# Attention and feed-forward on one core: the general path, which is passed over, takes its scores in three matmuls of 256 keys in place of two of 384

## The chip, the cores and the metric

The kernel runs on one core of a Trainium2 chip. A core has five engines that work beside each other, each with its own stream of instructions: TensorE (PE, matmuls and, as PEld, their weight loads), VectorE (DVE), ScalarE (ACT), GpSimd (POOL) and SyncE (SP, which issues transfers). They wait for each other through semaphores. The metric is the device time of one execution in microseconds (us), lower is better.

## The reference, cut to what matters

Four batches, eight heads, 768 positions, 64 numbers per head. Three of the eight heads see every earlier key; the other five see only the first four keys and a window of the last 64. The attention's output is joined over the heads to rows of 512 and goes through a feed-forward part that takes the maximum of two products.

```python
scores = scale * np.matmul(q, k.transpose(0, 1, 3, 2))
mask = np.where(retr, full_mask, stream_mask)          # per head
scores = np.where(mask, scores, -1000000000.0)
a = np.exp(scores - np.max(scores, axis=-1, keepdims=True))
a = a / (np.sum(a, axis=-1, keepdims=True) + 1e-09)
x = np.matmul(a, v)                                    # joined over heads: 3072 x 512
out = np.maximum(x @ w1, x @ w2) @ w_out
```

## The kernel before, in words

The kernel holds two programs for the same result.

The **fast path** (`tile_three_full_heads`) is written for three full heads and five windowed ones. It reads from `is_retrieval` which heads these are, sorts them, and addresses them through registers. Each batch is worked in two halves of 384 queries. For a half the queries and keys are cast and turned (L712), scores are made in blocks of 128 keys by 128 queries (L893), ScalarE takes the exponential (L912), VectorE masks it (L931), and TensorE multiplies with the values (L956). VectorE divides by the sums (L973, L983). The feed-forward part follows: w1 - w2 is formed once (L1122), its product with x is taken (L1177) and clipped at zero (L1201), and an output product adds this times w_out to x times a product of w2 and w_out (L1227). ScalarE or VectorE copies a tile of results (L480, L482), and a transfer stores it (L1246). The order of all this is not that of the text: a planner (`Order.run`) simulates the engines with given costs and emits the instructions in the order that it finds.

The fast path does not subtract the row's maximum before the exponential. So it ends with a judgement: VectorE checks that all reciprocal sums lie between 1e-12 and 1e12, TensorE adds up the checks (L1296), and VectorE (L1300 to L1307) writes one number, `verdict`, which is 1 if all are good and three heads are full.

The **general path** (`tile_any_heads`, from L1318 on) computes everything anew for any heads and any sums. For each batch, head and block of 128 queries it makes the scores of all 768 keys: matmuls into a tile of sums (L1407), each followed by a multiplication by scale and mask on VectorE (L1411). Then come the maximum, the exponential, the product with the values, and the feed-forward part.

What joins the two stands at the end of the program. Each engine loads the verdict into a register (L1581), and compares it (L1584):

```python
        right = nc.values_load(
            verdict, min_val=0, max_val=1, skip_runtime_bounds_check_because="a product of two flags"
        )
    with tc.If(right < 1):
        tile_any_heads(tc, *anyhow)
```

With verdict 1, as for the inputs used here, each engine jumps over the instructions of the general path. In its place stands a short block, also under L1584: it adds to the semaphores of the engines what the passed-over instructions would have added. Then comes the closing barrier (L1621, the line that opens the whole program): SP waits for all transfers and engines, each engine drains, GpSimd collects them and releases them, clears the semaphores, and once more collects and releases.

In each engine's stream the instructions stand in this order: fast path, general path, the short block, the closing barrier. TensorE passes over 9,803 instructions, VectorE over 3,165, GpSimd over 256, ScalarE over 136, and SP over one.

Of the kernel before, what the change touches and what calls it, by code (L numbers as in the profile page):

```python
# [11 lines left out]
F32 = mybir.dt.float32  # L12
# [1307 lines left out]
def tile_any_heads(tc, q, k, v, is_retrieval, w1, w2, wo, out, n_sink, window):  # L1320

    nc = tc.nc
    B, H, S, D = q.shape
# [3 lines left out]
    scale = 1.0 / float(D) ** 0.5  # L1327
# [8 lines left out]
        name="any_mask_table",  # L1336
# [5 lines left out]
    ps_s = pool("any_ps_s", 1, space=PSUM)  # L1342
# [9 lines left out]
        out=raw,  # L1352
# [9 lines left out]
    for name, src in (("any_w1", w1), ("any_w2", w2), ("any_wo", wo)):  # L1362
        n, cols = src.shape[0] // 128, src.shape[1]
# [9 lines left out]
    for b in range(B):  # L1373
        x = work.tile([128, NB, d_model], BF16, tag="x", name="any_x")
        for h in range(H):
            turned = []
            for name, src in (("any_q", q), ("any_k", k)):
                f = work.tile([128, NB, D], F32, tag="f", name="any_f")
                nc.gpsimd.dma_start(out=f, in_=src[b, h].rearrange("(n p) d -> p n d", p=128))
                fb = work.tile([128, NB, D], BF16, tag="fb", name="any_fb")  # L1380
                nc.vector.tensor_copy(out=fb, in_=f)
                pt = ps_t.tile([128, 1024], BF16, tag="t", name="any_pt")
                for i in range(NB):
                    nc.tensor.transpose(pt[0:D, i * 128:(i + 1) * 128], fb[:, i], ident)
                ft = work.tile([D, S], BF16, tag=name, name=name)
                nc.vector.tensor_copy(out=ft, in_=pt[0:D, 0:S])
                turned.append(ft)
            qt, kt = turned
            f = work.tile([128, NB, D], F32, tag="f", name="any_f")
            nc.gpsimd.dma_start(out=f, in_=v[b, h].rearrange("(n p) d -> p n d", p=128))  # L1390
            vb = work.tile([128, NB, D + 1], BF16, tag="vb", name="any_vb")
            nc.vector.memset(vb[:, :, D:D + 1], 1.0)
            nc.vector.tensor_copy(out=vb[:, :, 0:D], in_=f)
            for i in range(NB):
                if i % 3 == 0:
                    s3 = work.tile([128, 3, S], F32, tag="s", name="any_s")
                    a3 = work.tile([128, 3, S], BF16, tag="a", name="any_a")
                s = s3[:, i % 3]
                ps = ps_s.tile([128, 2, 512], F32, tag="s", name="any_ps")
                m = work.tile([128, S], F32, tag="m", name="any_m")  # L1400
                nc.vector.scalar_tensor_tensor(
                    out=m, in0=masks[:, 1, i], scalar=r[:, h:h + 1], in1=masks[:, 0, i],
                    op0=ALU.mult, op1=ALU.add,
                )
                for e in range(2):
                    cols = slice(e * S // 2, (e + 1) * S // 2)
                    nc.tensor.matmul(  # L1407
                        ps[:, e, 0:S // 2], lhsT=qt[:, i * 128:(i + 1) * 128], rhs=kt[:, cols],
                        start=True, stop=True,
                    )  # L1410
                    nc.vector.scalar_tensor_tensor(  # L1411
                        out=s[:, cols], in0=ps[:, e, 0:S // 2], scalar=scale, in1=m[:, cols],
                        op0=ALU.mult, op1=ALU.mult,
                    )
                nc.vector.tensor_scalar(
                    out=m, in0=m, scalar1=1e9, scalar2=-1e9, op0=ALU.mult, op1=ALU.add
                )
                nc.vector.tensor_tensor(out=s, in0=s, in1=m, op=ALU.add)
                top = work.tile([128, 1], F32, tag="top", name="any_top")
                nc.vector.tensor_reduce(out=top, in_=s, op=ALU.max, axis=AX.X)  # L1420
                nc.vector.tensor_scalar(
                    out=s, in0=s, scalar1=top, scalar2=None, op0=ALU.subtract
                )
                if i % 3 < 2:
                    continue
                nc.scalar.activation(out=a3, in_=s3, func=ACT.Exp)
                for n in range(3):
                    pt = ps_t.tile([128, 1024], BF16, tag="t", name="any_pt")
                    for j in range(NB):
                        nc.tensor.transpose(  # L1430
                            pt[:, j * 128:(j + 1) * 128], a3[:, n, j * 128:(j + 1) * 128], ident
                        )
                    at = work.tile([128, S], BF16, tag="at", name="any_at")
                    nc.vector.tensor_copy(out=at, in_=pt[:, 0:S])
                    po = ps_o.tile([128, 512], F32, tag="o", name="any_po")
                    for j in range(NB):
                        nc.tensor.matmul(
                            po[:, 0:D + 1], lhsT=at[:, j * 128:(j + 1) * 128], rhs=vb[:, j],
                            start=(j == 0), stop=(j == NB - 1),
                        )  # L1440
                    z = work.tile([128, 1], F32, tag="z", name="any_z")
                    nc.vector.tensor_scalar(
                        out=z, in0=po[:, D:D + 1], scalar1=1e-9, scalar2=None, op0=ALU.add
                    )
                    nc.vector.reciprocal(out=z, in_=z)
                    nc.vector.tensor_scalar(
                        out=x[:, i - 2 + n, h * D:(h + 1) * D], in0=po[:, 0:D], scalar1=z, scalar2=None,
                        op0=ALU.mult,
                    )
        for i in range(NB):  # L1450
            pt = ps_t.tile([128, 1024], BF16, tag="t", name="any_pt")
            for kc in range(KC):
                cols = slice(kc * 128, kc * 128 + 128)
                nc.tensor.transpose(pt[:, cols], x[:, i, cols], ident)
            xt = work.tile([128, KC, 128], BF16, tag="xt", name="any_xt")
            nc.vector.tensor_copy(out=xt, in_=pt[:, 0:d_model].rearrange("p (c t) -> p c t", c=KC))
            g = work.tile([128, FC, 128], BF16, tag="g", name="any_g")
            for fc in range(FC):
                both_ = []
                for wb in (w1b, w2b):  # L1460
                    ph = ps_o.tile([128, 512], F32, tag="o", name="any_ph")
                    for kc in range(KC):
                        nc.tensor.matmul(
                            ph[:, 0:128], lhsT=wb[:, kc, fc * 128:(fc + 1) * 128], rhs=xt[:, kc],
                            start=(kc == 0), stop=(kc == KC - 1),
                        )
                    both_.append(ph)
                h1 = work.tile([128, 128], F32, tag="h1", name="any_h1")
                nc.vector.tensor_copy(out=h1, in_=both_[0][:, 0:128])
                nc.vector.tensor_tensor(out=g[:, fc], in0=both_[1][:, 0:128], in1=h1, op=ALU.max)  # L1470
            pout = ps_o.tile([128, 512], F32, tag="o", name="any_pout")
            for fc in range(FC):
                nc.tensor.matmul(
                    pout, lhsT=g[:, fc], rhs=wob[:, fc], start=(fc == 0), stop=(fc == FC - 1)
                )
            ot = work.tile([128, d_model], F32, tag="ot", name="any_ot")
            nc.vector.tensor_copy(out=ot, in_=pout)
            r0 = b * S + i * 128
            nc.gpsimd.dma_start(out=out[r0:r0 + 128, :], in_=ot)
# [39 lines left out]
def kernel(  # L1519
# [19 lines left out]
    if not (1 <= window <= 64 and 0 <= n_sink <= 64):  # L1539
        tile_any_heads(tc, *anyhow)  # L1540
        return
# [42 lines left out]
    with tc.If(right < 1):  # L1584
        tile_any_heads(tc, *anyhow)
# [40 lines left out]
```

## Time and profile before

| what | value |
|---|---|
| median of three runs | 184.38 us |
| the three runs | 184.38, 184.33, 184.59 us |
| the profiled execution's own time | 183.78 us |
| its span, from the first to the last instruction | 180.9 us |
| mean granted clock of TensorE | 0.999 |
| verdict written (L1307) | 153.7 us after the span's start |
| last copy of results begins (L480) | 177.44 us |

The profile is of one execution. Its span is a little shorter than its time, since the time also takes in what lies around the first and last instruction. An engine is counted as busy while it computes; jumps, waits and the issuing of transfers are not counted as busy, but the view of a source line shows them with an engine's name and a q (PEldq, DVEq and so on), their durations, and when the first and the last of them began. The chain of waits is followed back from the last instruction that counts as work.

### The profile page before, as it was taken

What the parts mean: (1) busy time and instruction counts of PE and PEld (TensorE: products, weight loads), DVE (VectorE), ACT (ScalarE), POOL (GpSimd) and SP (SyncE); (2) the same over time, 40 slices, a digit from 0 to 9 for tenths busy, and PEclk for the clock granted to TensorE, in tenths of its full rate; (3) what the DMA queues carried; (4) which work ended last, traced back from release to release, by engine and by line L of the source; (5) the groups of instructions that cost most, each with busy time, mean ns of one, the idle gap of its engine ahead of it and who ended that gap; (6) DMA issues with size and microseconds to landing.
All of it is one profiled execution on the core that took longest, in us unless ns stands there. A gap on an engine that the chain in (4) does not pass through costs nothing.

```text
span 180.9 us, 4911 instructions
## 1 busy us (share of the span) xinstructions
PE 171.1 (95%) x1816; PEld 106.2 (59%) x1836; DVE 96.7 (53%) x283; ACT 131.7 (73%) x287; POOL 42.8 (24%) x77
## 2 busy tenths in 40 slices
PE   7899599989999999999999999999999999999992
PEld 7767486466747656565545565565466645545561
DVE  3456796599788985576247476656448500000000
ACT  3399695597999999999996984677798524525421
POOL 0000710100609488799671000000000000000000
PEclk9999999999999999999999999999999999999999
DMA  5999999999999999999999999160151052012013
GB/s 139 323 253 336 343 224 242 344 298 278 254 297 273 323 293 284 150 250 217 147 102 136 236 173 200 66 145 0 62 145 62 0 145 116 11 58 116 0 60 125
DMA packets 74929, 32.67 MB, mean 181 GB/s; under 512 B 54162, under 2 KB 71826, under 8 KB 74898
## 3 DMA queue, kind: packets, MB, share of 16 engines
q1 hardware_dynamic: 54704, 28.71, 64.9%
q0 software_dynamic: 19904, 3.41, 26.4%
q8 instruction: 16, 0.26, 0.6%
q10 hardware_dynamic: 290, 0.16, 0.3%
q14 instruction: 15, 0.12, 0.2%
HBM read 25.46 MB, written 6.29 MB: 176 GB/s over the span
## 4 chain that ended last, share of the span: by engine, by line
PE 73%; SPq 11%; DMA 6%; ACT 3%; DVE 3%; issue 2%; DVEq 0%; ACTq 0%
PE ps L1227 32%; PE ps L1177 24%; PE ps L893 7%; PE ps L956 7%; DMA ld<-in_v_dram 6%; SPq L523 5%; SPq L608 4%; PE ps L712 3%; ACT at L912 2%; SPq L513 2%; DVE w L1122 1%; SPq L595 1%; ACT qk L480 1%; DVE vx L482 1%; DVE vb L482 0%
## 5 line engine op out<-in xcount | busy, mean ns | idle before, releaser
L912 ACT ACTIVATE at<-ps 128x512 bf16<-128x512 f32 (+2 forms) x134 | 64.9, 595 | 3.5 <-PE ps L893 1.9
L1177 PE MATMUL ps<-xt,w 128*128 128x384 bf16 x256 | 46.0, 326 | 0.9 <-DVE w L1122 0.6
L1227 PE MATMUL ps<-wob,g 128*128 128x512 bf16 (+1 forms) x192 | 45.3, 370 | 0.4
L1177 PEld LDWEIGHTS <-w 128*128 128x128 bf16 x256 | 23.5, 98 | 15.9 <-issue 0.9
L1201 ACT ACTIVATE g<-ps 128x384 bf16<-128x384 f32 x56 | 27.5, 503 | 7.0 <-PE ps L1177 6.5
L931 DVE TENSOR_TENSOR at<-at,tab 128x1024 bf16<-128x1024 bf16 (+5 forms) x49 | 25.5, 537 | 12.7 <-ACT at L912 12.4
L1227 PEld LDWEIGHTS <-g 128*128 128x128 bf16 x200 | 18.1, 98 | 17.6 <-issue 0.2
L480 ACT COPY ot<-ps 128x512 f32<-128x512 f32 (+1 forms) x20 | 11.4, 572 | 22.8 <-PE ps L1227 22.7
L1227 PE MATMUL ps<-w2o,xt 128*128 128x512 bf16 (+1 forms) x91 | 24.2, 370 | 0.6
L956 PEld LDWEIGHTS <-at 128*128 128x128 bf16 x477 | 19.8, 97 | 7.3 <-issue 0.2
L983 DVE TENSOR_TENSOR x<-ps,rez 128x192 f32 x64 | 22.8, 356 | 1.8 <-DVE x L983 0.2
L956 PE MATMUL ps<-vb,at 128*128 128x65 bf16 x387 | 21.6, 193 | 0.0
L893 PE MATMUL ps<-qk 64*128 64x128 bf16 (+1 forms) x322 | 20.1, 230 | 0.3
L482 POOL CAST qb<-ld 128x384 bf16 x23 | 11.9, 551 | 35.5 <-DMA ld<-in_k_dram 35.5
L893 PEld LDWEIGHTS <-qk 64*128 64x128 bf16 x322 | 11.9, 94 | 11.2 <-issue 8.2
L1227 PEld LDWEIGHTS <-xt 128*128 128x128 bf16 x100 | 9.2, 98 | 8.8 <-issue 0.2
L480 ACT COPY qk<-ps 128x768 bf16<-128x768 bf16 x17 | 12.9, 817 | 0.6 <-PE ps L712 0.6
L471 PE MATMUL ps<-warmer 128*128 128x128 bf16 x147 | 12.1, 250 | 1.1 <-POOL warmer L1564 1.1
L712 PE MATMUL ps<-tab,qb 128*128 128x128 bf16 x144 | 10.4, 219 | 2.9 <-POOL qb L482 2.1
L480 ACT CAST qb<-ld 128x384 bf16 (+1 forms) x23 | 8.8, 452 | 5.1 <-DMA ld<-in_k_dram 3.1
L471 PEld LDWEIGHTS <-warmer 128*128 128x128 bf16 x147 | 10.9, 115 | 1.4 <-POOL warmer L1564 1.1
L712 PEld LDWEIGHTS <-qb 128*128 128x128 bf16 x144 | 8.4, 98 | 4.0 <-POOL qb L482 2.7
(62 smaller groups left out, 146.1 us busy)
## 6 DMA issues: line engine op xcount, KB each, us to landing
out_dram<-ot SPq DMA_DIRECT2D x23, 256.0 KB, 2.3
ld<-in_q_dram SPq DMA_DIRECT2D x6, 768.0 KB, 6.8
ld<-in_k_dram SPq DMA_DIRECT2D x6, 768.0 KB, 7.7
ld<-in_v_dram SPq DMA_DIRECT2D x18, 256.0 KB, 6.7
ld<-in_moe_w_dram SPq DMA_DIRECT2D x8, 512.0 KB, 8.2
wob<-in_moe_w_out_dram POOLq DMA_DIRECT2D x4, 256.0 KB, 8.5
ld<-in_q_dram POOLq DMA_DIRECT2D x8, 96.0 KB, 7.0
ld<-in_k_dram POOLq DMA_DIRECT2D x8, 96.0 KB, 7.2
```

The lines of the kernel that those rows point to most:

```text
L471: nc.tensor.matmul(banks[e][:, 0:128], lhsT=warm, rhs=warm, start=True, stop=True)
L480: nc.scalar.copy(out=out, in_=in_)
L482: eng[e].tensor_copy(out=out, in_=in_)
L712: nc.tensor.transpose(to[:, i], qbs[:, T["qb", n, hf] % NQB, t, i].rearrange("p h d -> p (h d)"), ident)
L893: nc.tensor.matmul(to.rearrange("p (i c) -> p i c", c=128), lhsT=lhsT, rhs=q_of(n, i, m)[rows], start=bk not in under, stop=True, skip_gro ...
L912: nc.scalar.activation(out=at[:, bk, 0:w], in_=bank(("ps", b, hf, t), part=bk)[:, 0:w], func=ACT.Exp, scale=scale,)
L931: eng[e].tensor_tensor(out=at, in0=at, in1=tbl, op=ALU.mult)
L956: nc.tensor.matmul(po[:, hh, i - NT * hf, :], lhsT=ats[:, T["at", b, hf, t] % NAT, bk, e * 128:(e + 1) * 128], rhs=rhs, start=first, stop= ...
L983: nc.vector.tensor_tensor(out=xs[:, (2 * b + hf) % NX, :, bass.ds(heads[2 * p + hh], 1), :], in0=po[:, hh, :, 0:D].unsqueeze(2), in1=z[:, ...
L1177: nc.tensor.matmul(bank(key)[:, 0:HALF], lhsT=w[:, kc, fc * 128:(fc + 1) * 128], rhs=xts[:, (2 * b + hf) % NXT, :, kc, :], start=(kc == 0) ...
L1201: nc.scalar.activation(out=g, in_=ph, func=ACT.Relu)
L1227: nc.tensor.matmul(bank(key)[:, cols], lhsT=lhsT, rhs=(w2o if kind == "x" else wob)[:, c, cols], start=(e == 0), stop=(e == len(steps) - 1),)
```

## The change

In the general path, the scores of a block of 128 queries are made in three pieces of 256 keys in place of two of 384. The tile of sums has the same size as before, 1024 numbers in each of 128 partitions; before, each half of 384 began at a multiple of 512, now the three pieces of 256 stand side by side in the first 768.

```diff
-                ps = ps_s.tile([128, 2, 512], F32, tag="s", name="any_ps")
+                ps = ps_s.tile([128, 1024], F32, tag="s", name="any_ps")
...
-                for e in range(2):
-                    cols = slice(e * S // 2, (e + 1) * S // 2)
+                for e in range(3):
+                    cols = slice(e * S // 3, (e + 1) * S // 3)
                     nc.tensor.matmul(
-                        ps[:, e, 0:S // 2], lhsT=qt[:, i * 128:(i + 1) * 128], rhs=kt[:, cols],
+                        ps[:, cols], lhsT=qt[:, i * 128:(i + 1) * 128], rhs=kt[:, cols],
                         start=True, stop=True,
                     )
                     nc.vector.scalar_tensor_tensor(
-                        out=s[:, cols], in0=ps[:, e, 0:S // 2], scalar=scale, in1=m[:, cols],
+                        out=s[:, cols], in0=ps[:, cols], scalar=scale, in1=m[:, cols],
                         op0=ALU.mult, op1=ALU.mult,
                     )
```

The general path is emitted 4 x 8 x 6 = 192 times for a block of queries, so the program holds 192 more matmuls, 192 more weight loads and 192 more multiplications on VectorE, all behind the comparison of L1584.

## The prediction

> **What bounds the kernel now.** I read the page's header and its chain first, then asked for the lines that the diff touches, then followed the last microseconds through the end of the timeline and the views of the source lines that close the program. The page:
>
> ```profile
> span 180.9 us, 4911 instructions
> PE 171.1 (95%) x1816; PEld 106.2 (59%) x1836; DVE 96.7 (53%) x283; ACT 131.7 (73%) x287; POOL 42.8 (24%) x77
> ...
> PE 73%; SPq 11%; DMA 6%; ACT 3%; DVE 3%; issue 2%; DVEq 0%; ACTq 0%
> PE ps L1227 32%; PE ps L1177 24%; PE ps L893 7%; PE ps L956 7%; DMA ld<-in_v_dram 6%; SPq L523 5%; SPq L608 4%; PE ps L712 3%; ACT at L912 2%; SPq L513 2%; DVE w L1122 1%; SPq L595 1%; ACT qk L480 1%; DVE vx L482 1%; DVE vb L482 0%
> ```
>
> TensorE is busy for 95% of the span and carries 73% of the chain, through the two output products (L1227, L1177). Before them stands a piece that waits for loads (DMA and SPq, 17%). Every line named lies in the fast path. The view of the source line of the changed matmul says:
>
> ```profile
> nothing on L1407; most used: ['L956', 'L893', 'L1227', 'L1177', 'L712', 'L471', 'L482', 'L912', 'L480', 'L983', 'L569', 'L1138', 'L1156', 'L1201', 'L931', 'L1246', 'L1086', 'L973', 'L1621', 'L523', 'L867', 'L1607', 'L513', 'L583', 'L1584']
> ```
>
> So the changed matmul isn't executed, and no line between L1318 and L1466 is among the most used. The end of the timeline, and from the view of the transfers the issue of the last store:
>
> ```profile
> 177.44 0.37 ACT L480 COPY ot<-ps 128x256 f32<-128x256 f32 x1 [0.89 <-PE ps L1227]
> 177.85 0.35 ACTq L1246 DMA_DIRECT2D out_dram<-ot  x1
> ```
> ```profile
> out_dram<-ot ACTq DMA_DIRECT2D x1, 128.0 KB, 1.8
> ```
>
> The last copy is followed by the last store, issued at 177.85 and landed 1.8 us on, at about 179.65. Beside that runs a second thing, the passing over itself. This is the view of L1584, the condition (start times in the fourth column):
>
> ```profile
> L1584 POOLq EVENT_SEMAPHORE  x4: 17/43/43, 157.0 to 157.3; - x4
> L1584 POOLq COMPARE_BRANCH  x1: 45/45/45, 154.2 to 154.2; - x1
> L1584 DVEq COMPARE_BRANCH  x1: 72/72/72, 154.3 to 154.3; - x1
> L1584 POOLq INC_SWDGE_SEM  x1: 422/422/422, 157.3 to 157.3; - x1
> L1584 DVEq EVENT_SEMAPHORE  x1: 21/21/21, 157.3 to 157.3; - x1
> L1584 PEldq COMPARE_BRANCH  x1: 3660/3660/3660, 175.9 to 175.9; - x1
> L1584 SPq COMPARE_BRANCH  x1: 53/53/53, 177.6 to 177.6; - x1
> L1584 ACTq COMPARE_BRANCH  x1: 54/54/54, 178.6 to 178.6; - x1
> L1584 ACTq EVENT_SEMAPHORE  x1: 17/17/17, 179.3 to 179.3; - x1
> L1584 PEldq EVENT_SEMAPHORE  x1: 51/51/51, 179.6 to 179.6; - x1
> ```
>
> Every engine evaluates the condition and jumps over the general path. SP, which has next to nothing to jump over, needs 53 ns. GpSimd stands from 154.2 to 157.0 and VectorE from 154.3 to 157.3; TensorE, which has by far the most to jump over, needs 3660 ns, from 175.9 to 179.6. Whether that matters is read from the closing barrier (L1621):
>
> ```profile
> L1621 SPq EVENT_SEMAPHORE  x14: 17/28/28, 177.8 to 180.8; - x14
> ...
> L1621 SPq DRAIN  x3: 7/7/13, 180.0 to 180.3; - x3
> L1621 DVEq DRAIN  x2: 10/14/17, 157.5 to 180.3; - x2
> L1621 ACTq DRAIN  x2: 8/8/8, 179.4 to 180.3; - x2
> L1621 PEldq DRAIN  x2: 8/8/8, 179.8 to 180.3; - x2
> ```
> ```profile
> SPq L1621 <- DMA out_dram<-ot: 1.5, 2, 1.2
> ```
>
> VectorE comes to the barrier at 157.5, ScalarE at 179.4, TensorE at 179.8, and SP, which first waits for the last store, at 180.0. So the store ends the program, and TensorE's jump is hidden behind it with only about 0.2 us to spare (two times rounded to 0.1, so 0.1 to 0.3). VectorE has 22.5 us to spare.
>
> **The change part by part.** In the program as built, the instructions ahead of the jump stand in the same order on all five engines, ScalarE, GpSimd and SP have the same number everywhere, and only the numbering of temporary registers differs. Behind the jump TensorE has 384 instructions more in the block that is passed over (192 matmuls and 192 weight loads: 4 batches x 8 heads x 6 blocks of queries, one more piece each) and VectorE 192 more. The terms:
>
> 1. Work executed: none added, none removed, 0 us. No queue, buffer, transfer or wait ahead of L1584 moves.
>
> 2. Constants that count the work passed over: in the branch not taken, TensorE and VectorE each add to a semaphore what the passed-over block would have added (4896 becomes 5088, 2754 becomes 2946), and two of SP's closing waits ask for values larger by 192. These four instructions are executed in both kernels, with another constant each: the 51 ns and 21 ns of L1584 and two of the 17 to 28 ns waits of L1621. Same number, same kind: 0 us.
>
> 3. The jump: TensorE's reaches 384 instructions further, VectorE's 192. What a longer jump costs, no row shows, so I bound it. From below: TensorE's could become as cheap as SP's (53 ns in place of 3660), and TensorE would stand at the barrier 3.6 us earlier; the store still lands when it does, so the span gains 0. From above: the price grows with the distance. Between SP's 53 ns over almost nothing and TensorE's 3660 ns over some 9,800 instructions, that is 0.37 ns each, or 0.14 us for 384 more, which is within the 0.2 us of cover. I take 0, because GpSimd passes over 256 instructions and takes 2.8 us (154.2 to 157.0) while VectorE passes over 3,165 and takes 3.0 us: past the first few hundred instructions the distance hardly counts. VectorE's own term is 0 at either end, with 22.5 us of cover. If TensorE's cover were gone, each further microsecond of its jump would be a microsecond of the program.
>
> 4. Placement: the code gets larger, and other data may come to lie elsewhere. No row shows an address. Its nearest measure is the spread of the three runs, 184.33 to 184.59: I allow 0.13 us to either side and take 0.
>
> Sum: 0 + 0 + 0 + 0 against the profiled execution's own 183.78 us, of which the span is 180.9 and 2.9 lie around it. The median of the runs shown, 184.38, is 0.60 above that execution; moved by the same sum it is **184.38 us**.
>
> The instruction queues on the page and, second, in the window from 177 to 181 us (packets, MB, share of the 16 transfer engines):
>
> ```profile
> q8 instruction: 16, 0.26, 0.6%
> ```
> ```profile
> q8 instruction: 2, 0.03, 3.4%
> q14 instruction: 2, 0.02, 1.3%
> ```
>
> Queue q8 brings code in pieces of 0.26 MB / 16 = 16 KB, and one takes 0.6% x 16 engines x 180.9 us / 16 = 1.09 us. Two of them fall in the last 4 us, so TensorE's long jump is a fetch of the code behind it, and another piece follows. [...]
>
> **The rivals.**
>
> *A border between two pieces of code falls just behind the landing (slower).* TensorE executes six instructions from its landing to the end: the semaphore of L1584, a jump, and two drains with two waits of L1621. If a border between pieces falls among them, TensorE must wait for one more piece before or inside the barrier, and everything waits for TensorE. Its price lies between one piece, 1.09 us, and a whole jump, 3.66 us, each less the 0.2 us of cover: 0.9 to 3.4 us. The nearest row is the whole jump, since VectorE's 3.0 us also show that most of a fetch is not the transfer: 184.38 + 3.4 = 187.8 us (185.3 at the low end). It decides from the point where TensorE's first drain comes after 180.0. For it: 384 more instructions move the landing, and the cover is thin. Against it: the landing can hit few places out of many; of the three long landings in this trace (TensorE, VectorE, GpSimd) none shows a second gap of that kind. 6 in 100.
>
> *Code behind the landing now arrives sooner (faster).* The last q8 piece could be one for which TensorE waits after the span, in the 2.9 us that lie around it. If that wait went, up to one piece would be saved: 184.38 - 1.1 = 183.3 us. For it: two q8 pieces lie in the last 4 us. Against it: inside the span it can gain nothing, as the store is later than TensorE; what lies around the span, no row shows. 6 in 100.
>
> *The change does reach executed work.* Were the general path run, its lines would stand in the profile. These rows price it, from the groups and from the groups of the last 6 us:
>
> ```profile
> L1177 PE MATMUL ps<-xt,w 128*128 128x384 bf16 x256 | 46.0, 326 | 0.9 <-DVE w L1122 0.6
> ```
> ```profile
> L1227 PE MATMUL ps<-wob,g 128*128 128x256 bf16 x16 | 2.1, 273 | 0.0
> ```
>
> Three matmuls of 256 columns take 3 x 273 = 819 ns, two of 384 take 2 x 326 = 652 ns: 192 x 167 ns = 32 us more on TensorE, 216 us were it all exposed. Nothing on L1407 speaks for it. 1 in 100.
>
> *Placement beyond the spread*, in either direction: 1 in 100, slower at 184.9.
>
> **How the numbers follow.** No measurable change 0.86 (within 0.2% of 184.38, 0.37 us, about what a measurement of this kernel can tell from no change); border behind the landing 0.06; general path reached 0.01; placement 0.01; code sooner 0.06. So faster 0.06, same 0.86, slower 0.08. The likeliest time is 184.38. The range from 184.0 to 184.8 holds the first case, with the 0.14 us of a jump that grows with its distance and the 0.13 us of placement; the 14 in 100 outside it may be left out.
>
> **What would show it.** If each step is right, the profile after has the same count of instructions on each engine, nothing on the lines of the general path, TensorE's jump near 3660 ns, its first drain before SP's, and the chain on the same lines with the same shares. The first rival would show as a TensorE drain or semaphore of L1621 or L1584 later than SP's with a further q8 piece before it. The second would show as an unchanged span with less around it. A jump that grows with the distance would show as about 3.8 us. I am wrong if the median leaves 184.0 to 184.8.

## The result, and the profile after

The changed kernel takes 183.31 us (median of 14 runs, 182.82 to 183.95) against 184.41 us before (median of 14, 183.59 to 185.78). The ratio is 0.9934, 95% interval 0.9914 to 0.9954: 0.66% faster, where no change was forecast. A second set of 10 runs gave 0.9937, 0.9907 to 0.9966. Two executions further on, of 187.79 us (VectorE +192) and 186.22 us (no general path), lie over 1.5% above the fastest of their kernel and are left out of its medians and ratio.

Of the profile after, the header and the engines' row:

```profile
span 181.5 us, 4931 instructions
PE 171.9 (95%) x1836; PEld 105.8 (58%) x1836; DVE 96.4 (53%) x283; ACT 131.8 (73%) x287; POOL 43.1 (24%) x77
```

The busy times are those of before to within 0.7%; the 20 additional TensorE rows are records that the trace before lacks. The span is *longer* than before, 181.5 against 180.9 us, and yet the profiled execution's own time is shorter, 183.38 against 183.78 us. So the gain isn't in the span at all. What lies around the span, time less span, went from 183.78 - 180.9 = 2.9 us to 183.38 - 181.5 = 1.9 us. It stands at 1.8 to 2.0 us in each of the 14 runs after. Below, "around the span" always means this difference.

The line of the condition (L1584) and the closing barrier (L1621), after:

```profile
L1584 DVEq COMPARE_BRANCH  x1: 72/72/72, 154.6 to 154.6; - x1
L1584 DVEq EVENT_SEMAPHORE  x1: 21/21/21, 157.5 to 157.5; - x1
...
L1584 PEldq COMPARE_BRANCH  x1: 3957/3957/3957, 176.3 to 176.3; - x1
L1584 SPq COMPARE_BRANCH  x1: 53/53/53, 177.9 to 177.9; - x1
...
L1584 PEldq EVENT_SEMAPHORE  x1: 51/51/51, 180.3 to 180.3; - x1
```
```profile
L1621 SPq DRAIN  x3: 7/7/13, 180.6 to 180.9; - x3
...
L1621 PEldq DRAIN  x2: 8/8/8, 180.4 to 181.0; - x2
...
L1621 PEldq EVENT_SEMAPHORE  x2: 51/51/51, 180.8 to 181.4; - x2
```

TensorE's jump is not shorter (3957 ns against 3660), and TensorE still comes to the barrier 0.2 us ahead of SP. Inside the span nothing was won.

### The profile page after: what moved, and what is told of

Its sections match the earlier page's. It is cut to its first block, busy times and chain, and to the rows that moved or that the text cites. A ratio compares the mean times of both kernels' runs of the same rounds, so it can differ in the third digit from the quotient of the medians.

```text
span 181.5 us, 4931 instructions
## 1 busy us (share of the span) xinstructions
PE 171.9 (95%) x1836; PEld 105.8 (58%) x1836; DVE 96.4 (53%) x283; ACT 131.8 (73%) x287; POOL 43.1 (24%) x77
## 4 chain that ended last, share of the span: by engine, by line
PE 60%; SPq 15%; DMA 14%; DVE 6%; ACT 2%; issue 1%; POOL 1%; POOLq 0%; DVEq 0%
PE ps L1227 29%; PE ps L1177 18%; DMA ld<-in_v_dram 7%; SPq L523 6%; PE ps L956 6%; PE ps L893 6%; DMA ld<-in_k_dram 4%; SPq L608 3%; SPq L513 3%; DMA ld<-in_q_dram 3%; DVE w L1122 3%; PE ps L712 1%; DVE vx L482 1%; SPq L595 1%; ACT at L912 1%
## 5 line engine op out<-in xcount | busy, mean ns | idle before, releaser
L1227 PE MATMUL ps<-wob,g 128*128 128x512 bf16 (+1 forms) x200 | 46.8, 371 | 0.0
L1227 PE MATMUL ps<-w2o,xt 128*128 128x512 bf16 (+1 forms) x100 | 24.8, 370 | 0.1
```

Of the source, the lines that this page charges most:

```text
L1227: nc.tensor.matmul(bank(key)[:, cols], lhsT=lhsT, rhs=(w2o if kind == "x" else wob)[:, c, cols], start=(e == 0), stop=(e == len(steps) - 1),)
```

## The experiments

The span of single executions wanders (for the kernel before from 180.8 to 182.4 us over 26 runs). What lies around it wanders too, from 2.6 to 3.3 us in the same runs, but stays well clear of the 1.8 to 2.0 us after the change. So each kernel is judged by that as well as by its time. Theory A: it matters where TensorE lands within the pieces in which its code arrives (on queue q8 before, 16 of 16 KB); before the change a border between pieces stands just behind the kernel's last instructions, and TensorE waits there, after the span. Rival B: the same on VectorE. Rival C: a larger program lies elsewhere in memory.

In all but the kernel without the general path and the two with a late store, only the passed-over part of the kernel before was altered; its result, had it been run, would have been the same. TensorE's part is made longer by repeating a matmul in N of the 192 blocks of queries, which adds 2N instructions (a weight load and a matmul each) to TensorE and none to the others:

```diff
                         start=True, stop=True,        # the matmul of L1407, in the kernel before
                     )
+                    if e and (b * H + h) * NB + i < N:
+                        nc.tensor.matmul(
+                            ps[:, e, 0:S // 2], lhsT=qt[:, i * 128:(i + 1) * 128], rhs=kt[:, cols],
+                            start=True, stop=True,
+                        )
                     nc.vector.scalar_tensor_tensor(
```

### Which engine's passed-over part, and has the step a period?

Four kernels on one chip: TensorE alone as in the change (N = 192, 384 instructions), VectorE alone as in the change, TensorE by 256 (N = 128), and no general path. The edits of the second and the fourth (`spare` is a single number, set up beside the verdict):

```diff
                 nc.vector.tensor_tensor(out=s, in0=s, in1=m, op=ALU.add)
+                nc.vector.tensor_copy(out=m, in_=s)
```
```diff
     with tc.If(right < 1):
-        tile_any_heads(tc, *anyhow)
+        nc.vector.memset(spare, 0.0)
```

> Only TensorE's passed-over part grows, by 384 instructions as in the change; VectorE's stays at 3,165. Theory A (the place where TensorE lands within its pieces of code sets what lies behind the span): as after, 183.3 us, with 1.9 us around the span. Rival B (VectorE's landing does it): as before, 184.4 us, 2.9 us around the span. Rival C (a larger program lies elsewhere in memory): something between or beyond, with no fixed 1.0 us.

> Only VectorE's passed-over part grows, by 192 instructions as in the change; TensorE's stays at 9,803. Theory A: as before, 184.4 us, 2.9 us around the span. Rival B: as after, 183.3 us, 1.9 us. Rival C: no fixed step.

> TensorE's passed-over part grows by 256 instructions, one whole piece of 16 KB if an instruction takes 64 bytes. Theory A: the landing keeps its place within the piece, so the time is as before, 184.4 us with 2.9 us around the span, although the program is larger. If only a longer jump or a larger program counts (rival C): nearer to after, 183.3 to 183.7 us.

> The general path is left out: what stands under the condition is one clearing of a number, so only the fast path's result is computed. Theory A: every engine's jump becomes short (TensorE's 3660 ns to about 50 to 100 ns), the last store still ends the span, near 181 us; around the span 1.9 us if no border follows the new landing, so 182.5 to 183.3 us. Rival C: the same span, but no telling what lies around it. If TensorE's jump were hidden for good, the span would not shorten by more than 0.3 us.

| kernel | runs | time, us | ratio to before, 95% | median span | around the span |
|---|---|---|---|---|---|
| before, same chip | 26 | 184.23 | | 181.25 | 2.9 |
| TensorE +384 | 6 | 182.89 | 0.9920 (0.9879 to 0.9962) | 181.2 | 1.7 |
| VectorE +192 | 9 | 184.40 | 1.0013 (0.9984 to 1.0041) | 181.3 | 3.1 |
| TensorE +256 | 10 | 184.10 | 0.9998 (0.9971 to 1.0025) | 181.15 | 2.9 |
| no general path | 8 | 182.98 | 0.9929 (0.9905 to 0.9953) | 181.3 | 1.7 |

TensorE's part alone makes the gain, VectorE's alone doesn't: rival B falls. Making the program larger by 256 instructions changes nothing: rival C falls too, and the step has a period that divides 256. The median spans differ by at most 0.15 us, so the spans carry none of the 1.2 us.

Without the general path, these are the condition (L1585 there) and the barrier (L1622):

```profile
L1585 PEldq COMPARE_BRANCH  x1: 223/223/223, 176.8 to 176.8; - x1
```
```profile
L1622 SPq DRAIN  x3: 7/7/13, 180.8 to 181.1; - x3
...
L1622 PEldq DRAIN  x2: 13/645/1277, 177.1 to 181.2; - x2
```

TensorE's jump falls from 3660 to 223 ns (50 to 100 had been expected) and it stands at the barrier 3.7 us ahead of SP, with a median span of 181.3 against 181.25 us: inside the span the jump was indeed hidden behind the last store.

### Where is the border?

Eight more values of N: the kernel with 128 more ran four times, the other seven once each.

> TensorE passes over 128 instructions more than before, so it lands at the same place within a piece of 256 as with 384 more, in a smaller program. Theory A: as after, 1.6 to 2.0 us around the span, about 183.1 us. Rival C: like the kernel with 256 more, 2.9 us, 184.1 us.

> 32 instructions more. Theory A says that the code that TensorE executes behind its landing reaches over a border; with 32 more the landing is either still ahead of that border (2.9 us around the span) or already behind it (1.7 us). Only if the border stands within the first six instructions behind the landing would the span itself grow, by 0.9 to 3.4 us.

> 64 instructions more: ahead of the border 2.9 us around the span, behind it 1.7 us; together with the kernel of 32 more it places the border to within 32 instructions.

> 192 instructions more, which is 64 short of a whole piece. Theory A: 2.9 us around the span if TensorE executes more than the distance from here to the next border (up to 64 more instructions than before are needed to stay ahead of it), 1.7 us if fewer. It bounds how much TensorE executes behind the landing.

> 8 instructions more than before. The border that 32 more pass lies less than 32 instructions behind the landing's place with 0 more. If it is still ahead: 2.9 us around the span. If it is passed: 1.7 us. If it stands within TensorE's six instructions between landing and end: the span itself grows, TensorE's drain comes after SP's wait for the store, and 185 to 188 us result.

> 16 instructions more: as for 8 more, one of three: 2.9 us around the span (border ahead), 1.7 us (border passed), or a span longer by 0.9 to 3.4 us (border within the six instructions).

> 24 instructions more: one of the same three. With 8 and 16 more, the border is placed to within eight instructions.

> 240 instructions more, 16 short of a whole piece: the landing lies 16 instructions further ahead of the border than before. 192 more, 64 further ahead, gave 1.7 us around the span, 256 more gave 2.9. If what TensorE executes reaches the border early enough to wait for it: 2.5 to 2.9 us; if it comes to it so late that the next piece is there: 1.7 us; between the two if the wait shrinks with the distance.

| TensorE's part longer by | time, us | span | around the span |
|---|---|---|---|
| 0 (before, profiled) | 183.78 | 180.9 | 2.9 |
| 8 | 184.18 | 182.4 | 1.8 |
| 16 | 183.30 | 181.6 | 1.7 |
| 24 | 182.94 | 181.2 | 1.7 |
| 32 | 182.86 | 181.2 | 1.7 |
| 64 | 182.84 | 181.2 | 1.6 |
| 128 (4 runs) | 182.69 | 181.0 | 1.7 |
| 192 | 185.16 | 183.5 | 1.7 |
| 240 | 183.07 | 181.4 | 1.7 |
| 256 (10 runs) | 184.10 | 181.15 | 2.9 |

With 128 more the ratio is 0.9912 (0.9886 to 0.9938). The wait exists only in a narrow stretch: at 0 and at 256, and no longer at 240 or at 8. A single execution can tell this, since around the span there were never under 2.5 us in the runs with 0 or 256 more, and never over 2.0 us in those of the other kernels of this table or after the change. The kernels with 8, 16, 24 and 240 more ran on another chip, where the kernel before, run once, took 183.73 us with 2.9 us around the span. The two times over 184 us with 1.7 to 1.8 us around the span are single executions in which TensorE came to its jump 1.0 and 2.6 us later than in the profile before; one execution can't tell more of these.

### Is it a wait in time, and can it be brought into the span?

Two kernels hold back the last store by six copies on ScalarE, one with TensorE's program untouched and one with 128 more. A third adds 4 instructions (N = 2). The fourth is the changed kernel once more, beside these on one chip.

```diff
+    late = keep.tile([128, d_model], F32, name="late")
...
                 def store(_, number=number, i=i, cols=cols, ends=ends):
                     r0 = b * S + i * 128
+                    for _ in range(6 if ends else 0):
+                        nc.scalar.copy(out=late, in_=ots[:, number % NOUT])
```

> The kernel before with six more copies on ScalarE ahead of the last store, which come to 3.4 us; TensorE's program is untouched and lands when it did, so the next piece of code, which starts some 0.7 us behind the landing and takes 1.1 us, is there before the barrier opens. Theory A as a wait in time: the span grows by about 3.4 us and 1.7 us stand around it, so 186.3 us. If the place has a fixed price: 2.9 us around the span, 187.5 us.

> The same late store with TensorE's passed-over part 128 instructions longer: by either reading 1.7 us around a span of about 184.6 us, 186.3 us. It is the scale for the kernel with the late store alone: equal to it if the border is a wait in time, 1.2 us less if it is a fixed price.

> 4 instructions more than before. 0 more waits behind the span, 8 more does not wait. If the border stands just behind TensorE's six last instructions, 4 more bring it in among them: TensorE would wait inside the barrier, the span would grow by 1 to 3 us (182.5 to 184.5 us) and 1.7 us stand around it. If the border is further on, 2.9 us around an unchanged span.

> The changed kernel beside the others on one chip. If VectorE's 192 more count for something: 1.9 us around the span, against 1.7 us in the kernels in which TensorE's part alone grew. If that was a difference between chips: 1.7 us.

| kernel | runs | time, us | ratio to before, 95% | median span | around the span |
|---|---|---|---|---|---|
| before, same chip | 21 | 184.37 | | 181.4 | 3.0 |
| late store | 6 | 186.12 | 1.0094 (1.0064 to 1.0123) | 184.45 | 1.7 |
| late store, TensorE +128 | 2 | 186.81 | 1.0115 (1.0053 to 1.0178) | 185.15 | 1.7 |
| TensorE +4 | 6 | 185.97 | 1.0073 (1.0023 to 1.0122) | 184.3 | 1.7 |
| the changed kernel | 10 | 183.63 | 0.9937 (0.9907 to 0.9966) | 181.7 | 1.9 |

With the late store the span grows by 3.05 us and the time by only 1.75: what lies around the span falls to 1.7 us although TensorE lands where it always did. So the border has no fixed price; TensorE waits for a piece that is on its way, and a later end covers the wait. With 128 more beside the late store nothing further is won: the same 1.7 us around the span, and 186.81 us in two runs against 186.12.

With 4 more instructions the wait moves to where the profile can see it. The closing barrier of that kernel (L1626 there), and what SP waited for at the end:

```profile
L1626 SPq DRAIN  x3: 7/7/13, 180.7 to 181.0; - x3
L1626 DVEq DRAIN  x2: 10/14/17, 157.9 to 181.0; - x2
L1626 ACTq DRAIN  x2: 8/8/8, 179.7 to 181.0; - x2
L1626 PEldq DRAIN  x2: 8/8/8, 180.5 to 183.9; - x2
L1626 PEldq EVENT_SEMAPHORE  x2: 51/51/51, 180.9 to 184.1; - x2
```
```profile
SPq L1626 <- PEq L1626: 3.3, 2, 3.1
```

TensorE's first drain and first wait pass at 180.5 and 180.9, and the others make their second drain at 181.0. TensorE's second comes at 183.9, 2.9 us late, and all wait for it (SP's longest wait on TensorE is 3.1 us, against 0.5 us before). Between those two TensorE instructions stands the border. The piece shows on q8, which moved one inside TensorE's jump before and after, and none from 177 us on in the kernel without the general path. Here it is from 181.5 to 182.5 us:

```profile
q8 instruction: 1, 0.02, 5.8%
```

It begins at 181.55 and takes 5.8% x 16 x 1 us = 0.93 us, so it has arrived at 182.5, and TensorE goes on 1.4 us later. The same 1.4 us lie between the arrival of the piece that moves inside TensorE's jump and the jump's end, before (178.2 and 179.6) and after (178.8 and 180.2). With 1.4 us, as an estimate, the last piece of the kernel before (begun at 180.3, arrived at 181.4) is of use at 182.8 us, 1.9 us behind the span's end, and that of the kernel with the late store (arrived at 181.65) at 183.1 us, ahead of its span's end at 184.0. That only 1.2 of those 1.9 us show in the time would mean that the rest is hidden beside what follows every span; this is argued.

By the program TensorE executes six instructions from its landing: semaphore, jump, drain, wait, drain, wait (the jump leaves no row in the profile). So with 4 more the border stands behind the fourth, with 0 more behind the eighth, two instructions past the kernel's own, and with 8 more the landing is the first instruction of the new piece. The whole table above follows: with 240 more the border is 24 instructions behind the landing, and no wait is seen.

## Why the prediction was wrong

1. *What bounds the kernel*: right. TensorE and the last store set the span, and the median spans of before and after differ by 0.3 us at most (181.4 and 181.7 on one chip).

2. *No work executed, constants only, 0 us*: right; nothing else moved in the span.

3. *The jump, "I take 0"*: this is the step that failed. Its bound from below said that, however TensorE's jump turned out, "the store still lands when it does, so the span gains 0". That holds, as the kernel without the general path shows. But the sum then carried the 2.9 us around the span over as a constant, without a row that shows them to be one, and there sat the gain: they fell to 1.9 us. TensorE's cover at the barrier was taken for cover to the end of the program; it ends with the span, and TensorE, as is argued below, has more to execute behind it.

4. *A jump that grows with its distance*, allowed for with 0.14 us: not to be seen. TensorE's jump took 3660 ns over 9,803 instructions, 3553 over 10,187 (TensorE +384), and 3957 and 4077 over the same 10,187 in the changed kernel's two profiles. With TensorE's program untouched two traces give 3660 and 4060 ns (before and the late store), so a term of 0.14 us could not have been told from none.

5. *Rival "code behind the landing now arrives sooner"*: this is what happened, and it had 6 in 100. That its time, 183.3 us, agrees with the 183.31 measured is luck: its 1.1 us were the transfer of one piece, whereas what went was 1.2 us of a longer wait, less 0.2 us that VectorE's part added. The rows to rate it higher were at hand: 2.9 us around the span, and a second piece of code in the last 4 us. A narrower window would have said more. Instruction queues from 180.0 to 181.0 us, before:

```profile
q8 instruction: 1, 0.02, 7.0%
```

One piece begins in that microsecond and takes 7.0% x 16 x 1 us = 1.12 us. It cannot have arrived when the span ends at 180.9: a transfer of code in flight, with no instruction left in the span that could need it. By the place of the border found above, TensorE needed it two instructions later. After the change a piece begins in that microsecond too, and 1.9 us stand around the span:

```profile
q8 instruction: 1, 0.02, 5.8%
```

6. *Rival "a border just behind the landing"* is the same mechanism with the other sign. It doesn't occur at 384 more, but at 4 more it does: span 2.9 us longer (forecast 0.9 to 3.4), time 1.6 us longer (184.37 to 185.97), since the wait around the span goes at the same time.

7. *VectorE's term, "0 at either end"*: right for the span. Around it, VectorE's 192 more cost 0.2 us: 3.1 against 2.9 us when added alone, and 1.9 against 1.7 us in the changed kernel (24 runs on two occasions) over the kernel with TensorE's 384 alone. The gain of 1.1 us is thus TensorE's 1.2 less VectorE's 0.2, to within the rounding.

8. *What would show it*: the second rival was to show as "an unchanged span with less around it", and did. The chain's shares were not a good witness: PE stands at 73% of the chain before, and the changed kernel's two profiles give 60% and 70%, so they vary from one execution to the next.

The length of a piece in instructions: 256 more restored the old time (184.10 us, 2.9 us around the span) while 128 more did not (182.69 us, 1.7 us). Before, ahead of TensorE's jump at 175.9 us, q8 shows

```profile
q8 instruction: 14, 0.23, 0.6%
```

while the page has 1,816 + 1,836 = 3,652 matmuls and weight loads, some 261 for each of the 14 pieces. So, as an estimate from these runs and rows, a piece of 16 KB holds 256 instructions, 64 bytes each, as was assumed for the kernel with 256 more. A border close behind a landing cost 1.2 us behind the span here and 2.9 us inside it.

Shown are the engine, the period (once, from 0 to 256), the border's place and that it is a wait in time. Only argued is that TensorE's instructions behind the span belong to the closing code that follows every program here, since the profile ends with the span. Open is what VectorE's 0.2 us are. Why TensorE's jump takes 3.55 to 4.08 us in six traces (before, after, the changed kernel once more, TensorE +384 and +4, the late store), in no order of its length, the transfers of two show: a piece begins 1.2 us behind the jump's start, takes 1.08 us before and 1.34 us after, and the jump ends 1.4 us behind its arrival. Why one transfer takes longer than another stays open.

## What to carry to other kernels

Code that is never executed still decides where the code behind it lies: after a long jump close to the end of a program, look whether a border between fetched pieces falls into the last few instructions, and shift it if it does, and measure again: 8 instructions were enough here, and 4 made it worse. Put the time beside the span before reading anything else; a gain or loss that no view of the span shows lies around it, and the difference of the two, whose values with and without the wait never overlapped here, tells it sooner than the noisy total. The lowest median of these versions run more than once is that of the kernel before with 128 unexecuted TensorE instructions more, 182.69 us, which keeps TensorE's 1.2 us and leaves VectorE where it was; that it beats the changed kernel too rests on 1.7 against 1.9 us around the span, as the intervals of the ratios overlap; the kernel with 384 more on TensorE alone (182.89 us) can't be told from it.

## What the runs showed of the hardware

- A jump over 9,803 to 10,187 instructions held TensorE for 3.55 to 4.08 us in six traces, and the jump that is left without the general path for 0.22 us. SP's took 0.05 us.
- A piece of TensorE's code was 16 KB (0.26 MB in 16 on q8), which is 256 instructions as an estimate from the runs with 256 and 128 more. It took 0.9 to 1.1 us to transfer in the three windows shown of single pieces and 1.34 us inside the jump after; TensorE went on some 1.4 us behind its arrival. With the border four instructions behind the landing TensorE came 2.9 us late, of which the transfer was 0.93 us.
- The same unexecuted code moves the time by -0.9% to +0.7%, depending on its length alone (128 and 4 instructions more), more than the 0.2% that was taken for the least that can be told from no change.
